# Routing moved to the beginning of a step, one sequence routed in halves, and first loads in halves, in an attention and top-1 expert kernel

## The chip, the cores and the metric

The kernel runs on one core of a Trainium2 chip. The metric is the device time of one execution in microseconds (us), as the median of several runs. All numbers of the profile come from one profiled execution of the same program.

## What is computed

Four sequences of 768 tokens with 8 heads of 64 go through an attention in which a token sees the first `n_global` (8) keys and the last `n_local` (96) keys, with a bias that grows with distance. The result, 3072 rows of 512, goes through 8 experts; each row goes to the one whose gate is highest.

```python
keep = is_global | is_local
scores = scale * q @ k.T - slopes * dist          # where keep, else -1e9
a = exp(scores - max); a = a / (sum(a) + 1e-9)
x = (a @ v) as rows of 512
logits = x @ w_gate;  e = argmax(logits);  gate_w = softmax(logits)[e]
out[row] = gate_w * (relu(x[row] @ w1[e]) @ w2[e])
```

## The kernel before

**Who orders the work.** A recorder (`Flow`) takes the instructions in the order in which the program names them, puts each into its engine's queue in that order, and derives from the tiles what each has to wait for. So each engine works its own queue strictly in program order: TensorE (PE), VectorE (DVE), ScalarE (ACT), GpSimd (POOL), and SP, which issues most DMAs. PSUM is told apart by bank: an engine that writes a bank waits for the others that read it.

**The attention as a pipeline of 24 steps.** Each sequence has 6 blocks of 128 tokens; step n (`steps`, L1087) begins block n and carries earlier blocks on. In PE's order a step has: `scores(n)` (L491, two key blocks for each query block, one for the first of a sequence), `values(n - 1)` (L528), `sums(n - 2)` (L543, the sums of the weights and the gate's logits), the transposes `q_in` and `k_in` of block n + 2 (L475, L467), `tokens_x(n - 2)` (L550) and `tokens_u(n - 2)` (L553). DVE adds the bias to the scores in two halves (`weigh`, L501), makes the logits of block n - 3 (`normal`, L562 to L566) between the two, and its rows (`rows`, L571). ACT takes exponents (L509) and copies what PE wrote: values (L531), sums (L545), and the transposed q and k (L477, L469). POOL adds the two halves of the weights (`both`, L515) and puts the first 32 keys and values of the sequence into a block (L1096, L1152). SP loads q and k four steps ahead (`loads`, L375) and v three steps ahead (`load_v`, L380).

**Routing.** When the last block of a sequence has its logits, step n with n - 3 = 5, 11, 17 ends with `choose` (L584 to L589, the best expert of each token) and `gates` (L594 to L598). In the next step, after the first `weigh`, PE counts how many earlier tokens of the sequence chose the same expert (`counts`, L605 to L610); after `rows` DVE turns that into row numbers (`slots`, L618 to L623), and six `scatter`s (L627, an indirect DMA of POOL that sends a block's 128 rows to their experts' regions) are queued, one a step; for sequence 2, whose slots come in step 21, all six are issued at the end of that step. `load_x(0)` (L779), the load of the first expert's rows, stands in SP's queue behind all scatters of sequences 0 to 2. Also in step 21 `early_counts` (L1184 and the table L733 to L743) writes down the first expert's count. Sequence 3 is routed within the first expert's products.

**Other work in the steps.** From step 5 on, eight weight loads of the first expert (L690, L693), one a step; from step 13 on eight sums of its weight quarters on DVE (`w_sums`, L710 to L713), one a step, also in steps 14 and 20, which choose.

**The beginning.** SP loads q and k of block 0 whole, then q, k and v of the next blocks. ACT's queue loads `n_global` and `n_local` spread over 128 partitions (L400, L401) and the gate weights (L419). Seven small DVE operations make floats of the two numbers (`numbers`, L389 to L395); then the masks and biases follow. Before step 0, block 0 is transposed; step 0 transposes blocks 1 and 2.

**The experts.** After step 23 (`values(23)`, the last sums) the experts' products (L842 and others) fill PE up to the end.

Of the kernel before, what the change touches and what calls it, by code (L numbers as in the profile page):

```python
# [13 lines left out]
F32 = mybir.dt.float32  # L14
BF16 = mybir.dt.bfloat16
I32 = mybir.dt.int32
# [308 lines left out]
class Attention:  # L325
# [12 lines left out]
    def __init__(self, f, dims, psum, arena, small, keep):  # L338
# [29 lines left out]
        self.top, self.se, self.slot = a.many(3, self.NBLK)  # L368

# [14 lines left out]

    def numbers(self):

        f, k = self.f, self.keep
        words, part_i, part_f, num = k["words"], k["part_i"], k["part_f"], k["num"]
        f.dve.tensor_copy(out=part_i[:, 0, :], in_=words[:, :, 1])  # L389
        f.dve.tensor_scalar(part_i[:, 1, :], words[:, :, 0], 16, None, ALU.logical_shift_right)  # L390
        f.dve.tensor_scalar(part_i[:, 2, :], words[:, :, 0], 0xFFFF, None, ALU.bitwise_and)
        f.dve.tensor_copy(out=part_f[:], in_=part_i[:])
        f.dve.tensor_scalar(num[:], part_f[:, 0, :], 4294967296.0, None, ALU.mult)
        f.dve.scalar_tensor_tensor(num[:], part_f[:, 1, :], 65536.0, num[:], ALU.mult, ALU.add)
        f.dve.tensor_tensor(num[:], num[:], part_f[:, 2, :], ALU.add)  # L395

    def constants(self):
        f, k, P, E = self.f, self.keep, self.P, self.E

        f.act.dma_start(out=k["words"][:, 0, :], in_=self.n_global.bitcast(I32).partition_broadcast(P))  # L400
        f.act.dma_start(out=k["words"][:, 1, :], in_=self.n_local.bitcast(I32).partition_broadcast(P))  # L401
# [14 lines left out]
        wg = self.w_gate.rearrange("(c p) e -> p c e", p=P)  # L416
        for a in range(2):
            r = slice(64 * a, 64 * a + 64)
            f.act.dma_start(out=self.wgbd[r, :, E * a:E * a + E], in_=wg[r])  # L419
# [14 lines left out]
    def masks(self, kinds):  # L434

        V, k = self.f.dve, self.keep
        ng, nl = k["num"][:, 0:1], k["num"][:, 1:2]
# [25 lines left out]
    def k_in(self, n, bank):  # L463
        f, pt = self.f, self.psum[:, bank, :].rearrange("p (m c) -> p m c", m=4)
        raw = self.raw_k[n % 3]
        for m in range(4):
            f.pe.transpose(pt[:, m, :], raw[:, 2 * m:2 * m + 2, :].rearrange("p a d -> p (a d)"),  # L467
                           self.keep["ident"][:])
        return lambda: f.act.copy(self.kt[n % 3], pt)  # L469

    def q_in(self, n, bank):
        f, pt = self.f, self.psum[:, bank, :].rearrange("p (m c) -> p m c", m=4)
        raw = self.raw_q[n % 3]
        for m in range(4):
            f.pe.transpose(pt[:, m, :], raw[:, 2 * m:2 * m + 2, :].rearrange("p a d -> p (a d)"),  # L475
                           self.keep["ident"][:])
        return lambda: f.act.activation(self.qt[n % 2], pt, AF.Copy, bias=0.0, scale=0.125)  # L477
# [99 lines left out]
    def choose(self, b):  # L577

        f, k, V = self.f, self.keep, self.f.dve
        xr, lg = self.xr[b % 2], self.lg[b % 2]  # L580
        shape = [128, self.NBLK, self.E]
# [1194 lines left out]
```

## Time and profile before

| | |
|---|---|
| time, median of 3 runs | 508.08 us (507.99 to 508.6) |
| profiled execution, its own time | 509.14 us |
| its span, first to last instruction | 507.3 us |
| PE, DVE, ACT, POOL busy | 94%, 70%, 34%, 32% of the span |
| mean granted TensorE clock | 0.984 |

In the profile L12 is line 12 of the kernel. `PE` is a matmul, `PEld` its weight load. A row of a timeline has its start, its length, the engine, line, operation, what it writes and reads, how many instructions it merges, and in brackets how long the engine was idle ahead of it and what ended that; "issue" there is a wait that the profile shows nothing for. A busy PE is not a PE at its peak: starts are recorded, ends are modelled. The steps can be read off PE's first L491 of each:

| step | begins at us | lasts us |
|---|---|---|
| 0, 1, 2 | 9.93, 15.54, 20.43 | 5.61, 4.88, 7.00 |
| 3, 4, 5 | 27.42, 33.67, 39.91 | 6.24, 6.24, 6.25 |
| 8, 9, 10 | 57.53, 63.77, 70.40 | 6.24, 6.63, 6.47 |
| 14, 15, 16 | 94.49, 100.73, 108.30 | 6.24, 7.56, 6.51 |
| 17, 18, 19 | 114.81, 121.05, 126.43 | 6.24, 5.38, 6.06 |
| 20, 21, 22 | 132.49, 138.73, 146.29 | 6.24, 7.56, 11.40 |
| 23 | 157.69 | 8.80 to the values of block 23 |

### The profile page before, as it was taken

Reading aid. Unit: us, or ns where it says so; the run is one execution under the profiler, and the core shown is the slowest. Engines: PE = TensorE matmul, PEld = TensorE weight load, DVE = VectorE, ACT = ScalarE, POOL = GpSimd, SP = SyncE. Lnnn points to the kernel's source line nnn. Section 1 sums busy time; section 2 is a strip of 40 time slices with the busy share of each in tenths; the row PEclk is TensorE's granted clock in tenths of the full one; section 3 lists DMA queues with packets and bytes.
Section 4 is the critical chain, followed back from the end, with each engine's and each line's share of the span. In section 5 each row is a group of like instructions: output and inputs, shape, how many; then the busy total and the mean of one; then the engine's idle time right before and its main releaser. Section 6 shows DMA issues by size and latency. Waiting matters only on the chain. (4 is left out here: it accounts for less than half of the span.)

```text
span 507.3 us, 10785 instructions
## 1 busy us (share of the span) xinstructions
PE 476.9 (94%) x4397; PEld 452.2 (89%) x4397; DVE 352.8 (70%) x626; ACT 174.0 (34%) x306; POOL 163.4 (32%) x192
## 2 busy tenths in 40 slices
PE   3999999999987999999999999999999999999990
PEld 3888888888875799999999999999999999999880
DVE  4655685898892785576868877777877776777830
ACT  3666656546543231213214214104214204303310
POOL 1545466668665143300203304303304303003011
PEclk9999999999997999999999999999999999999996
DMA  9999999999516246989756666568467479001000
GB/s 152 210 236 250 185 212 236 239 218 219 124 74 158 87 172 148 234 186 255 158 169 178 143 211 148 127 164 210 103 201 193 96 194 232 3 1 62 6 25 29
DMA packets 120344, 79.24 MB, mean 156 GB/s; under 512 B 86422, under 2 KB 103318, under 8 KB 120272
## 3 DMA queue, kind: packets, MB, share of 16 engines
q1 hardware_dynamic: 112960, 63.77, 57.6%
q0 software_dynamic: 6480, 14.45, 8.2%
q8 instruction: 51, 0.84, 0.7%
q14 instruction: 21, 0.17, 0.1%
q10 hardware_dynamic: 832, 0.02, 0.1%
HBM read 61.39 MB, written 23.71 MB: 168 GB/s over the span
## 5 line engine op out<-in xcount | busy, mean ns | idle before, releaser
L842 PE MATMUL psum<-arena 128*128 128x208 f32 (+5 forms) x1776 | 291.4, 325 | 1.1 <-DVE arena L874 0.9
L842 PEld LDWEIGHTS psum<-arena 128*128 128x128 f32 x1776 | 285.4, 190 | 3.3 <-DVE arena L874 1.9
L832 POOL DMA_INDIRECT out_dram<-arena,to x16 | 21.5, 1344 | 171.9 <-ACT arena L824 147.2
L501 DVE TENSOR_TENSOR arena<-psum,arena 128x1024 f32<-128x1024 f32 x40 | 48.8, 1219 | 36.4 <-PE psum L491 36.2
L515 POOL TENSOR_TENSOR arena<-arena 128x512 f32<-128x512 f32 x40 | 53.3, 1334 | 35.2 <-ACT arena L509 35.2
L509 ACT ACTIVATE arena<-arena 128x1024 f32<-128x1024 f32 (+1 forms) x48 | 47.4, 987 | 47.9 <-DVE arena L501 36.3
L491 PE MATMUL psum<-arena 64*128 64x128 f32 x704 | 50.4, 291 | 1.0 <-ACT arena L477 0.7
L491 PEld LDWEIGHTS psum<-arena 64*128 64x128 f32 x704 | 45.2, 198 | 5.7 <-issue 3.4
L866 ACT ACTIVATE arena<-arena 128x512 f32<-128x512 f32 x48 | 30.2, 630 | 53.4 <-DVE arena L901 21.6
L528 PE MATMUL psum<-arena 128*64 128x128 f32 x704 | 44.5, 279 | 0.3 <-issue 0.3
L528 PEld LDWEIGHTS psum<-arena 128*64 128x64 f32 x704 | 38.7, 139 | 3.3 <-issue 0.7
L870 ACT COPY arena<-psum 128x512 f32<-128x512 f32 (+1 forms) x24 | 13.5, 561 | 81.8 <-PE psum L842 81.6
L755 POOL DMA_INDIRECT xg_dram<-small,pad x24 | 23.4, 974 | 52.5 <-ACT arena L879 41.5
L627 POOL DMA_INDIRECT xg_dram<-arena,slot_i x24 | 24.7, 1030 | 23.3 <-DVE arena L911 15.8
L885 DVE TENSOR_TENSOR arena<-arena,psum 128x512 f32<-128x512 f32 (+1 forms) x24 | 15.8, 659 | 23.0 <-PE psum L842 21.0
L911 DVE TENSOR_TENSOR arena<-arena,psum 128x512 f32<-128x512 f32 x24 | 16.5, 688 | 17.7 <-PE psum L842 17.2
L906 DVE TENSOR_TENSOR arena<-arena,psum 128x512 f32<-128x512 f32 x24 | 16.5, 688 | 14.7 <-PE psum L842 13.4
L901 DVE TENSOR_TENSOR arena<-arena,psum 128x512 f32<-128x512 f32 x24 | 16.5, 688 | 12.8 <-PE psum L842 11.5
L467 PE MATMUL psum<-ident,arena 128*128 128x128 f32 x96 | 16.1, 294 | 8.8 <-DMA arena<-in_k_dram 7.3
L832 POOL DMA_INDIRECT out_dram<-ylast,to x17 | 17.4, 1024 | 21.1 <-ACT ylast L824 12.7
L713 DVE TENSOR_TENSOR arena<-arena 128x1024 f32<-128x1024 f32 x16 | 19.9, 1242 | 3.0 <-issue 2.9
L874 DVE TENSOR_TENSOR arena<-arena,psum 128x512 f32<-128x512 f32 (+1 forms) x24 | 15.8, 657 | 8.5 <-PE psum L842 8.1
(152 smaller groups left out, 534.7 us busy)
## 6 DMA issues: line engine op xcount, KB each, us to landing
arena<-in_moe_w_dram SPq DMA_DIRECT2D x64, 512.0 KB, 6.3
arena<-xg_dram SPq DMA_DIRECT2D x64, 128.0 KB, 8.5
arena<-in_q_dram SPq DMA_DIRECT2D x24, 256.0 KB, 3.5
arena<-in_k_dram SPq DMA_DIRECT2D x24, 256.0 KB, 5.1
arena<-in_v_dram SPq DMA_DIRECT2D x24, 256.0 KB, 7.7
xg_dram<-arena SPq DMA_DIRECT2D x2, 1032.0 KB
xg_dram<-arena,slot_i POOLq DMA_INDIRECT x24, 5.4
xg_dram<-small,pad POOLq DMA_INDIRECT x24, 9.3
```

The lines of the kernel that those rows point to most:

```text
L491: f.pe.matmul(self.psum[:, 2 * g + a, c:c + P], lhsT=kt[r, m, :], rhs=qt[r, m, :], start=True, stop=True, skip_group_check=True)
L501: f.dve.tensor_tensor(e, s, self.bias[:, g, :, 1:3, :].rearrange("p h k c -> p h (k c)"), ALU.add)
L509: f.act.activation(e, e, AF.Exp)
L515: f.pool.tensor_tensor(self.es[n % 3][:, g], e[:, :, 0:P], e[:, :, P:2 * P], ALU.add)
L528: f.pe.matmul(po[r, m, :], lhsT=self.v[(n - ab) % 6][:, 2 * m + a, :], rhs=self.e[n % 2][:, m // 2, 2 * a + m % 2, P * ab:P * ab + P], sta ...
L627: self.f.pool.indirect_dma_start(out=self.xs[:], out_offset=bass.IndirectOffsetOnAxis(ap=k["slot_i"][:, b % 2, u:u + 1], axis=0), in_=self ...
L713: lambda: V.tensor_tensor(c["t4"], c["b21"], c["t2"], ALU.subtract)]
L755: self.f.pool.indirect_dma_start(out=self.xs[:], out_offset=bass.IndirectOffsetOnAxis(ap=self.keep["pad"][:, g, j:j + 1], axis=0), in_=sel ...
L832: return pool.indirect_dma_start(out=self.out[:], out_offset=bass.IndirectOffsetOnAxis(ap=self.keep["to"][:, g, j:j + 1], axis=0), in_=sel ...
L842: f.pe.matmul(self.psum[:, bank, 256 * t + cut.start:256 * t + cut.stop], lhsT=w[k][:, ts(t, 128)], rhs=x[k][:, cut], start=(fresh and t = ...
L866: f.act.activation(d, d, act)
L901: V.tensor_tensor(dst["c22"], u3, bank(W), ALU.add)
```

## The change

- **Routing at the beginning of the step behind the choice.** In a step that takes slots, `normal`, `counts` and `slots` now come straight behind the scores, before the first `weigh`.
- **Sequence 2 in halves.** Its blocks 12 to 14 are chosen in step 17 and blocks 15 to 17 in step 20; slots follow in steps 18 and 21. Scatters go two a step while more than three are waiting, else one; what is left in step 21 goes ahead of that step's `both`. `early_counts` moves from step 21 to step 22. The weight sums run from step 12 on and skip the steps that choose.
- **First loads in halves.** q and k of block 0 come in four heads each, k on SP and q on ACT, and are transposed and copied in halves. The two numbers come to one partition; a matmul with ones spreads them (`near`), and the old seven operations run later, one a step, on that partition. The gate weights move from ACT's queue to SP's, behind the first v. Seven matmuls of zeros (`zeros`) go ahead of the first transposes.
- **The next blocks turned behind the scores.** Blocks 2 and 3 are transposed right behind the scores of steps 1 and 2, with ACT's copies ahead of `exponent`.

The diff, cut to what the text speaks of:

```diff
+    def first_loads(self):
+        f, k, P = self.f, self.keep, self.P
+        f.act.dma_start(out=k["words"][0:1, 0, :], in_=self.n_global.bitcast(I32).partition_broadcast(1))
+        f.sp.dma_start(out=k["words"][0:1, 1, :], in_=self.n_local.bitcast(I32).partition_broadcast(1))
+        for half in range(2):
+            r = slice(4 * half, 4 * half + 4)
+            for on, t, src in ((f.sp, self.raw_k[0], self.k), (f.act, self.raw_q[0], self.q)):
+                on.dma_start(out=t[:, r, :], in_=src[0, r, 0:P, :].rearrange("h p d -> p h d"))
+    def zeros(self, bank, count):
+        for _ in range(count):
+            self.f.pe.matmul(self.psum[:, bank, 0:self.P], lhsT=self.kg.rearrange("p a c -> p (a c)"), rhs=self.us,
+                             start=True, stop=True, skip_group_check=True)
+    def near(self, bank):
+        f, k = self.f, self.keep
+        f.dve.tensor_copy(out=self.low[0:1], in_=k["words"][0:1, :, 0])
+        f.pe.matmul(self.psum[:, bank, 0:2], lhsT=self.kg.rearrange("p a c -> p (a c)"), rhs=self.low,
+                    start=True, stop=True, skip_group_check=True)
+        f.dve.tensor_copy(out=k["near"][:], in_=self.psum[:, bank, 0:2])
...
     def constants(self):
-        f.act.dma_start(out=k["words"][:, 0, :], in_=self.n_global.bitcast(I32).partition_broadcast(P))
-        f.act.dma_start(out=k["words"][:, 1, :], in_=self.n_local.bitcast(I32).partition_broadcast(P))
+        f.dve.memset(self.kg, 1.0)
+        f.dve.memset(self.us, 0.0)
+        f.dve.memset(self.low, 0.0)
...
-        at.loads(0)
+        at.first_loads()
+        at.constants()
         at.loads(1)
         at.load_v(0)
         at.loads(2)
         at.load_v(1)
-        at.load_v(2)
-        at.constants()
+        at.gate_weights()
+        at.zeros(SK, 6)
         at.masks_first()
-        at.numbers()
-        at.k_in(0, T0)()
-        at.q_in(0, T1)()
+        at.near(SK)
+        at.zeros(SK, 1)
+        for pairs, kb, qb in ((slice(0, 2), T0, T1), (slice(2, 4), O, U)):
+            kk, qq = at.k_in(0, kb, pairs), at.q_in(0, qb, pairs)
+            kk()
+            qq()
         at.masks(slice(0, 1))
...
         at.loads(3)
+        at.load_v(2)
+        numbers = at.numbers()
+        whole, half = slice(0, NBLK), NBLK // 2
+        units = {NBLK * b + NBLK - 1: (b, whole) for b in range(B - 2)}
+        units[NBLK * (B - 2) + half - 1] = B - 2, slice(0, half)
+        units[NBLK * (B - 2) + NBLK - 1] = B - 2, slice(half, NBLK)
...
+            if n == 2:
+                kk, qq = at.k_in(3, T0), at.q_in(3, U)
+                kk()
+                qq()
-            if n + 4 < N:
+            if n + 4 < N and n != 1:
                 at.loads(n + 4)
             if n + 3 < N:
                 at.load_v(n + 3)
+            unit = routed.pop(n - 4, None)
+            if unit:
+                at.normal(n - 3, U)
+                at.counts(T1, unit[1])
+                at.slots(*unit, T1)
+                scat.extend((unit[0], u) for u in range(unit[1].start, unit[1].stop))
             at.weigh(n, 0)
+            if n == 1:
+                values_first = at.values(0, O)
+                kk, qq = at.k_in(2, U), at.q_in(2, T0)
+                kk()
+                qq()
+                at.loads(5)
             at.exponent(n, 0)
...
-            if n >= 3:
+            if n >= 3 and not unit:
                 at.normal(n - 3, U)
...
-            if n - 4 in routed:
-                at.counts(T1)
+            if n == N - 3:
+                for s in scat:
+                    at.scatter(*s)
+                scat.clear()
             at.weigh(n, 1)
             at.exponent(n, 1)
...
-            if bb is not None:
-                at.slots(bb, T1)
-                scat.extend((bb, u) for u in range(NBLK))
             us = at.sums(n - 2, U) if n >= 2 else None
-            if bb == B - 2:
+            if n == N - 2:
                 early_counts()
             kk = qq = None
-            if n + 2 < N and bb is None:
+            if 2 <= n and n + 2 < N:
                 qq = at.q_in(n + 2, T1)
-            if n + 2 < N:
                 kk = at.k_in(n + 2, SK)
             if n >= 2:
                 at.tokens_x(n - 2, T0)
-            if n + 2 < N and bb is not None:
-                qq = at.q_in(n + 2, T1)
...
+            if n >= 3 and numbers:
+                numbers.pop(0)()
...
-            if n >= 3 and (n - 3) % NBLK == NBLK - 1:
-                at.choose((n - 3) // NBLK)
-                at.gates((n - 3) // NBLK)
-                routed[n - 3] = (n - 3) // NBLK
-            if n >= 13 and w0_sums:
+            if n - 3 in units:
+                unit = routed[n - 3] = units[n - 3]
+                at.choose(*unit)
+                at.gates(*unit)
+            elif n >= 12 and w0_sums:
                 w0_sums.pop(0)()
-            for _ in range(NBLK if b == B - 1 and i >= 3 else 1):
+            for _ in range(2 if len(scat) > half else 1):
                 if scat:
                     at.scatter(*scat.pop(0))
```

`choose`, `gates`, `counts` and `slots` take the range of blocks as an argument and are otherwise the same. In step 21 the copy of the first values on POOL goes ahead of the scatters. The program that runs only when the numbers are out of range makes its own floats of them.

## Prediction, made before the change was run

> **What bounds the kernel now.** I read the slices first, then the windows of single steps, then the timelines of the engines in the one step that stands out, and the waits at the start.
>
> ```profile
> PE   3999999999987999999999999999999999999990
> PEclk9999999999997999999999999999999999999996
> ```
>
> A slice is 12.7 us. TensorE is full nearly everywhere, so the time is TensorE's queue plus its holes. There are two: the first slice, and slices 12 and 13 (140 to 165 us), where the granted clock falls too. The change touches both places. A step n begins where its scores (L491) begin on PE; these are steps 20, 21, 22, 23 (up to the values of block 23), and the half-clock stretch (columns: start:end, us, busy of each engine, clock, DMA share, GB/s).
>
> ```profile
> 132.49:138.73 6.24, 6.24 (x102) 5.58 (x101) 4.96 (x13) 3.96 (x8) 5.05 (x6) 1.00 0.13 45
> 138.73:146.29 7.56, 6.84 (x114) 5.93 (x113) 7.25 (x19) 3.32 (x6) 4.65 (x6) 1.00 0.10 37
> 146.29:157.69 11.40, 6.99 (x95) 5.13 (x94) 5.44 (x18) 4.63 (x8) 8.42 (x9) 0.93 0.37 141
> 157.69:166.49 8.80, 8.12 (x94) 7.11 (x94) 3.90 (x9) 2.75 (x4) 3.32 (x4) 0.70 0.65 120
> 156.13:162.96 6.83, 5.67 (x49) 5.23 (x51) 3.04 (x6) 2.16 (x4) 2.42 (x3) 0.50 0.77 163
> ```
>
> 6.24 us with PE busy 6.24 is the undisturbed step. Step 21, which takes slots at its end, costs 7.56; step 22 costs 11.40 although it has no transposes of q and k. In step 22 POOL issues all six scatters of sequence 2 in a row; PE and ACT stand meanwhile:
>
> ```profile
> 147.76 1.01 POOL L627 DMA_INDIRECT xg_dram<-arena,slot_i  x1 [0.81 <-DVE ki L740]
> ...
> 154.24 0.98 POOL L627 DMA_INDIRECT xg_dram<-arena,slot_i  x1 [0.30 <-issue]
> ```
> ```profile
> 155.04 0.59 ACT L531 COPY arena<-psum 128x512 f32<-128x512 f32 x1 [4.49 <-PE psum L543]
> ```
> ```profile
> 153.52 0.27 PE L543 MATMUL psum<-arena 128*32 128x128 f32 x1 [1.05 <-issue]
> 153.72 0.82 PE L550 MATMUL psum<-ident,arena 128*128 128x128 f32 x4
> 157.29 0.47 PE L553 MATMUL psum<-ident,arena 128*128 128x128 f32 x1 [2.74 <-ACT arena L545]
> 157.69 3.79 PE L491 MATMUL psum<-arena 64*128 64x128 f32 x32
> ```
>
> ACT's copy of the values waits 4.49 us for PE, although PE's records put the values' end at 150.47. Then the exponent and the sums' copy follow late, and PE's last transpose waits 2.74 us for that. The scores then take 3.79 instead of 2.06. Which part of a scatter holds PE the trace does not say; that it happens under six of them in a row, it does.
>
> At the start PE waits for the first K block, then runs long at a slow clock (16 score records in 2.08 us here, 32 in 2.06 later):
>
> ```profile
> 7.27 1.12 PE L467 MATMUL psum<-ident,arena 128*128 128x128 f32 x4 [7.27 <-DMA arena<-in_k_dram]
> 8.18 1.06 PE L475 MATMUL psum<-ident,arena 128*128 128x128 f32 x4
> 9.93 2.08 PE L491 MATMUL psum<-arena 64*128 64x128 f32 x16 [0.69 <-ACT arena L477]
> ```
>
> **What the Trainium skill says.** "TensorE: Matmul & The Clock Gate", Part 1, has the array at half clock until it was busy through a free-running window of 3.41 us, and again after an idle one. The trace agrees: half clock for 6.83 us, two windows, after PE had 1.02 us of work in 152.72 to 156.13. "SBUF — State Buffer", section "SBUF: two separate sides", says that VectorE in a two-port mode and GpSimd lock each other out of one port pair for a whole instruction. The trace agrees: the cast to slot_i (L623) took 1.14 us at 69.75, ending with POOL's sum at 70.86, and 0.17 at 181.90 with POOL idle. The same section says that TensorE never waits for a DMA at SBUF. The 4.49 us above speak at least against leaning on that. "DMA: Bandwidth & Descriptors", "Anatomy of one DMA", gives a GpSimd DMA about 2 us of completion; here the last scatter leaves POOL at 155.22 and SP's waiting load goes at 157.28.
>
> **The change, part by part.**
>
> *The six scatters of step 22 (gain).* Sequence 2 is now routed in halves: blocks 12 to 14 are chosen in step 17 and get slots in step 18; blocks 15 to 17 in steps 20 and 21. By the new rule (two scatters a step when more than three wait) the first three are out by step 20. The last three go in step 21, before the two sums on POOL, and step 22 has none. Step 22 without the stall: scores 1.98, values 1.90, sums 0.79, tokens_x 0.44, tokens_u 0.2, 5.3 on PE; but the last transpose waits for DVE, ACT: in step 4 (33.67) the sums' copy starts at +5.44, and in step 22 ACT also copies first_v (0.50), so 5.94 + 0.25, the step 6.45. Step 23 likewise 5.95. Before: 11.40 and 8.80. Gain 4.95 + 2.85 = 7.8, of which some 2.5 are the half clock (scores 1.73, values 0.73). The bounds: nothing, if the stall has another cause, and 7.8.
>
> *Slots at the beginning of a step (cost).* In steps 9, 15, 18, 21 DVE now does normal, waits for counts, does slots, and only then weigh. Behind that wait stand both weighs and rows; ACT's exponents and the sums' copy wait for them, and PE's last transpose for that copy. Counts follow the scores: 1.98 + 0.45 (67.66 to 68.11) = +2.43. Choose of the step before ends at +1.42 (65.19 against 63.77) and normal takes 0.88, to +2.3: not late. Slots 0.88 (181.12 to 181.98; the cast 0.17, since POOL has just its copy of keys then), weigh 0 at +3.3, its exponent +4.57, the values' copy +5.53, exponent 1 +6.01, the sums' copy +6.97 to +7.21, the last transpose +7.26: 7.45 in all. Before, step 9 and 10 took 6.63 + 6.47, 15 and 16 7.56 + 6.51 (one w0_sum stood ahead of their weighs), 18 5.38, 21 7.56. After: 7.45 + 6.24 twice, 5.8 (a first block, half as wide, bounded by choose and normal), 7.2 (three blocks, fewer counts). Differences +0.6, -0.4, +0.4, -0.35: +0.25. Upper bound: the cast waits for POOL each time, 4 x 0.97, +4.1; lower -0.6.
>
> *Scatters elsewhere.* Two a step: POOL 2 x 1.3 + 3.4 = 6.0, under 6.24; a sum that comes late is read two steps later. Zero. In step 21 the sums on POOL shift by 3.9 us and are read in step 23: zero. SP's load of x (7.5 us) starts at 3.3 + 3.9 + 2.0 = +9.2 in step 21 instead of 157.28 (+18.6), ready at +16.7, needed at +21: off the path both times. The early counts' table (nine small DVE operations, 146.89 to 148.24) moves to step 22, the w0_sums from steps 13 to 20 to 12 to 22. DVE in step 22: rows end +5.0, table +6.4, sum +7.5, next weigh needed at 6.45 + 1.21 = +7.66: hidden by 0.2, else their excess counts.
>
> *Start (gain).* The two words go to one partition instead of 128, gate weights behind V, q and k in halves on two queues. By +5 us the DMA engines had moved only 57 GB/s x 5 = 285 KB, then 216 KB a us. Without the small pieces I take 512 KB from 3.3 on at 216: first halves at 4.9, second at 6.1 (bounds 5.2, and 7.2 as now). Then 4 transposes of the second half, 0.9: scores(0) at 7.0 instead of 9.93 (8.1 at the bound). The near chain (one copy, matmul, copy instead of seven DVE operations of 0.2) is ready before. The seven go one a step from step 3 into DVE's idle 2.5 us: zero, 0.2 each otherwise. Seven zero matmuls wait for nothing of weight; they fill under half a window, so no clock.
>
> *The next blocks' transposes (part loss).* Blocks 2 and 3 now stand right behind the scores of steps 1 and 2, with their ACT copies ahead of exponent. From 7.0: scores 2.0, eight slow transposes 1.95, a hole of 0.8 for the copies (0.59 each), scores(1) 11.8, PE busy from there. The clock comes 3.4 to 6.8 later, 15.3 to 17 mostly. Scores(1) 3.8, values 1.0 to 1.7, transposes 1.0, hole 0.75: scores(2) 18.3 to 19.1. Scores 2.0, transposes 1.0, values 1.9, sums 0.8, transposes 0.95, the rest 0.7: scores(3) at 25.7 to 26.5, against 27.42. Gain 1.4; bounds 0.4 (loads as late as now) and 3.2 (clock by 12.8, as would be if a window four fifths full is enough).
>
> **Sum.** -7.8 + 0.25 - 1.4 = -8.95. The profiled execution took 509.14 (span 507.3, 1.8 around it), 1.06 above the median 508.08; that execution becomes 500.2, the median 499.1. From the experts on PE is full and everything only shifts.
>
> **Rivals.**
> *The stall follows the scatters* into step 21. For: three in a row remain. Against: the burst at 182.85 to 190.7 leaves PE's matmuls at their rate, and step 15 with one scatter shows none. 4.5 us over five scatters is 0.9 each: 1.8 to 2.7 for three, 499.1 + 2.7 = 501.8; with a half-clock window behind it (2.5) 504.3.
> *The start comes out well, the clock early*: 3.2 instead of 1.4, 497.3. For: the zeros and an earlier busy run. Against: 9.36 to 12.77 was over four fifths busy and did not raise the clock.
> *The change misses the cause*: step 22 stalls as before though no scatter is in it: 499.1 + 7.8 = 506.9. Against: ACT is released at 155.01, as the burst ends.
> *Slower*: the new chain counts, slots, weigh, exponent, copy, on which PE waits in four steps. Price: each us beyond my +3.3 for slots' end costs 4 us; it decides from 2.2 us a step (8.95 / 4). For: DVE's casts took 1.14 under POOL. Against: that explains 0.97, a total of +3.9 and 503.0; more is not in sight. Slower would be 510.
>
> **Chances.** Forecast as worked out, 497.8 to 500.8: 0.58. Early clock (496 to 497.8): 0.12. Stall follows, or slots cost their bound (500.8 to 504.5): 0.21. Cause missed: 0.05. Slower: 0.03; the rest ends within 0.2% (1.0 us, about what can be told from no change): 0.01. The 8-in-10 range is 496.3 to 503.2. Faster 0.95, same 0.02, slower 0.03.
>
> **What would show it.** After: no PE or ACT wait over 1 us in step 22, clock 1.00 from the warm-up to the end of attention; steps 9, 15, 21 near 7.45 with the last transpose waiting for ACT's sums' copy; slots' cast 0.17; scores(0) near 7.0, scores(3) near 26. Wrong, if step 21 holds a PE hole over 1 us under its scatters, or weigh starts after +4 in the four steps, or scores(3) is not before 27.

## The result, and the profile after

The changed kernel took 500.77 us as a median (500.38 to 501.62), the kernel before, run beside it, 508.03 (507.76 to 508.6): a ratio of 0.9858, with an interval of 0.9841 to 0.9875. The forecast was 499.1, its range 496.3 to 503.2. The profiled execution took 500.38, its span 498.5, against 509.14 and 507.3. The total came out close; its parts did not.

New line numbers for the same things: scores L519, weigh L529, exponent L537, sums on POOL L543, values L556 and their copy L559, sums on PE L571 and their copy L573, tokens_x L578, tokens_u L581, choose L612 to L616, slots L646 to L651, scatter L655, weight sums L738 to L741, the early table L761 to L771, the first expert's rows L807 and L816, its matmuls L870.

The slices first, as they were shown of before:

```profile
PE   7999999999997999999999999999999999999990
PEclk9999999999999999999999999999999999999996
```

The first slice has risen from 3 to 7 tenths, the hole in slices 12 and 13 is one slice of 7, and the clock is never taken back before the end. Then the windows of steps 20, 21, 22, 23, up to the values of block 23:

```profile
131.29:137.53 6.24, 6.24 (x102) 5.58 (x101) 4.96 (x13) 3.96 (x8) 5.04 (x6) 1.00 0.12 46
137.53:144.87 7.34, 7.00 (x109) 5.80 (x108) 6.90 (x19) 3.51 (x7) 4.77 (x6) 1.00 0.20 74
144.87:151.38 6.51, 5.66 (x95) 4.74 (x94) 5.05 (x15) 4.22 (x8) 5.87 (x6) 1.00 0.38 123
151.38:158.75 7.37, 5.72 (x95) 4.75 (x94) 5.71 (x13) 2.74 (x4) 3.80 (x4) 1.00 0.53 108
```

Step 22 is 6.51 where it was 11.40, but step 23 has PE busy for only 5.72 of 7.37. And PE's beginning (the zeros L399, the spread of the two numbers L406, the halves of k and q L495 and L503, scores of block 0):

```profile
1.42 2.93 PE L399 MATMUL psum<-arena 128*128 128x128 f32 x12 [1.42 <-DVE arena L432]
4.14 0.43 PE L406 MATMUL psum<-small,arena 128*128 128x2 f32 x2
...
5.14 0.38 PE L495 MATMUL psum<-ident,arena 128*128 128x128 f32 x2
...
6.51 1.26 PE L519 MATMUL psum<-arena 64*128 64x128 f32 x16
```

Six zeros kept PE busy for 2.93 us (a matmul of this type has two records); the clock's records show full speed from 4.63 us on (16.18 before), and the 16 score records take 1.26 us where they took 2.08.

Laid out by stages, both profiled executions:

| stretch | before | after | difference | forecast |
|---|---|---|---|---|
| start to scores(3) | 27.42 | 22.30 | -5.12 | -1.4 |
| steps 3 to 20 | 111.31 | 115.23 | +3.92 | +0.6 |
| step 21 | 7.56 | 7.34 | -0.22 | -0.35 |
| step 22 | 11.40 | 6.51 | -4.89 | -4.95 |
| step 23 | 8.80 | 7.37 | -1.43 | -2.85 |
| values(23) to the end | 340.80 | 339.78 | -1.02 | 0 |
| sum | 507.29 | 498.53 | -8.76 | -8.95 |

The +3.92 is steps 9 (7.89 for 6.63), 11 and 12 (+0.5 together), 16 (7.29 for 6.51), 17 (6.99 for 6.24) and 18 (6.12 for 5.38). So the question for the experiments is fourfold: what the start is worth and why; what the steps from 9 to 18 lose; whether the row of six scatters was the cause in step 22; and what of the tail remains. The experiments come in four groups; the kernels of one group ran on one chip. The kernel before took 507.98 to 510.19 us on these chips, so totals of different chips can't be compared: the steps in the profiles carry the verdicts, and the ratios, each against the kernel before on the same chip, support them.

### The profile page after: what moved, and what is told of

It reads as the page before. It is cut to its first block, busy times and chain, and to the rows that moved or that the text cites. A ratio compares the mean times of both kernels' runs of the same rounds, so it can differ in the third digit from the quotient of the medians.

```text
span 498.5 us, 10842 instructions
## 1 busy us (share of the span) xinstructions
PE 474.9 (95%) x4413; PEld 450.0 (90%) x4413; DVE 356.1 (71%) x646; ACT 173.2 (35%) x309; POOL 164.7 (33%) x192
## 5 line engine op out<-in xcount | busy, mean ns | idle before, releaser
L870 PE MATMUL psum<-arena 128*128 128x208 f32 (+5 forms) x1776 | 290.8, 325 | 1.0 <-DVE arena L902 0.8
L870 PEld LDWEIGHTS psum<-arena 128*128 128x128 f32 x1776 | 285.5, 190 | 2.6 <-DVE arena L902 1.3
L860 POOL DMA_INDIRECT out_dram<-arena,to x16 | 22.5, 1403 | 171.9 <-ACT arena L852 147.2
L529 DVE TENSOR_TENSOR arena<-psum,arena 128x1024 f32<-128x1024 f32 x40 | 48.3, 1219 | 29.4 <-PE psum L519 29.4
L537 ACT ACTIVATE arena<-arena 128x1024 f32<-128x1024 f32 (+1 forms) x48 | 47.4, 988 | 47.5 <-DVE arena L529 40.2
L543 POOL TENSOR_TENSOR arena<-arena 128x512 f32<-128x512 f32 x40 | 51.9, 1300 | 30.9 <-ACT arena L537 30.5
L519 PE MATMUL psum<-arena 64*128 64x128 f32 x704 | 46.4, 280 | 1.6 <-ACT arena L505 1.6
L519 PEld LDWEIGHTS psum<-arena 64*128 64x128 f32 x704 | 41.8, 187 | 5.2 <-issue 2.5
L556 PE MATMUL psum<-arena 128*64 128x128 f32 x704 | 43.7, 276 | 0.3 <-issue 0.3
L556 PEld LDWEIGHTS psum<-arena 128*64 128x64 f32 x704 | 37.9, 137 | 2.9 <-issue 0.6
L655 POOL DMA_INDIRECT xg_dram<-arena,slot_i x24 | 25.4, 1058 | 21.9 <-DVE arena L939 16.2
L741 DVE TENSOR_TENSOR arena<-arena 128x1024 f32<-128x1024 f32 x16 | 21.1, 1321 | 1.3 <-issue 1.1
L738 DVE TENSOR_TENSOR arena<-arena 128x1024 f32<-128x1024 f32 x16 | 19.4, 1211 | 1.9 <-DMA arena<-in_moe_w_dram 1.9
```

The costliest lines, as they stand in the source:

```text
L519: f.pe.matmul(self.psum[:, 2 * g + a, c:c + P], lhsT=kt[r, m, :], rhs=qt[r, m, :], start=True, stop=True, skip_group_check=True)
L529: f.dve.tensor_tensor(e, s, self.bias[:, g, :, 1:3, :].rearrange("p h k c -> p h (k c)"), ALU.add)
L537: f.act.activation(e, e, AF.Exp)
L543: f.pool.tensor_tensor(self.es[n % 3][:, g], e[:, :, 0:P], e[:, :, P:2 * P], ALU.add)
L556: f.pe.matmul(po[r, m, :], lhsT=self.v[(n - ab) % 6][:, 2 * m + a, :], rhs=self.e[n % 2][:, m // 2, 2 * a + m % 2, P * ab:P * ab + P], sta ...
L655: self.f.pool.indirect_dma_start(out=self.xs[:], out_offset=bass.IndirectOffsetOnAxis(ap=k["slot_i"][:, b % 2, u:u + 1], axis=0), in_=self ...
```

## Experiments: the two halves of the change

**start_only** is the changed kernel with the routing of before; **routing_only** the kernel before with the routing of the change (sequence 2 in halves, slots ahead of weigh, two scatters a step). start_only differs from the changed kernel by

```diff
-            unit = routed.pop(n - 4, None)
-            if unit:
-                at.normal(n - 3, U)
-                at.counts(T1, unit[1])
-                at.slots(*unit, T1)
...
+            if bb is not None:
+                at.slots(bb, whole, T1)
+                scat.extend((bb, u) for u in range(NBLK))
...
-            for _ in range(2 if len(scat) > half else 1):
+            for _ in range(NBLK if b == B - 1 and i >= 3 else 1):
```

and what belongs to it; routing_only differs from the kernel before by the same lines the other way round.

> Only the start of the change: first loads in halves, the spread of the two numbers, the zeros, blocks 2 and 3 turned behind the scores; the routing stands where it stood before (six scatters in a row in step 22). In the changed kernel's trace scores(3) begin at 22.30 us instead of 27.42. Theory (the start alone is worth 5.1 us and nothing later takes it back): scores(3) at 22.3, steps 22 and 23 at 11.4 and 8.8 as before, time 508.0 - 5.1 = 502.9. Rival (the prediction's own account, the start is worth 1.4 and the rest of what the trace shows there is given back in later steps): 506.6.

> Only the routing of the change (sequence 2 in halves, slots ahead of the first weigh, two scatters a step while more than three wait); the start stands as before. Theory (the steps from 3 to 23 took 139.07 us before and 136.45 in the changed kernel, so the routing is worth 2.6 only: 6.3 won in steps 22 and 23, 3.7 lost in steps 9 to 21): 508.0 - 2.6 = 505.4, with step 10 at 6.4, 16 at 7.3, 17 at 7.0, 22 at 6.5. Rival (the prediction's own account: 7.8 less 0.25): 500.5.

Measured: start_only 0.9942 (0.9919 to 0.9965), 507.0 us against 510.19; scores(3) at 22.62, step 22 at 12.82, step 23 at 7.84. routing_only 0.9927 (0.9910 to 0.9943), 506.25 us; step 10 at 6.48, 16 at 7.33, 17 at 7.01, 22 at 6.51.

The routing is worth 3.7 to 4 us, nearer to the theory's 2.6 than to the prediction's 7.55. The start brings scores(3) 4.8 earlier, but only 3 us of it reach the end: in this profile step 22's stall was 1.4 longer, and steps 12 and 13 took 6.16 and 6.28 instead of 5.38 and 6.0; of the first, 0.49 us are waits of PE's transposes for the loads of q and k. Such waits between scores(3) and step 23 come to 0.2 to 4.4 us in five of the ten profiles with the new start, and to 0.31 in one of the four with the old: PE has come closer to its loads, it seems. So the theory overrated what the start gives in the end, and the prediction underrated what it gives at scores(3).

## Experiment: without the zeros

```diff
-        at.zeros(SK, 6)
...
-        at.zeros(SK, 1)
```

> The changed kernel without its seven matmuls of zeros. Theory (the zeros raise the clock: they keep PE busy from 1.4 to 5, and the records show full speed from 4.63 on): without them the clock comes at 13 to 17 us, scores(3) begin at 25 to 26.5 instead of 22.3, time 503.5 to 505. Rival (the earlier loads would bring the clock anyway, or the records of the start mislead): scores(3) within 0.5 of 22.3, time 500.8 to 501.3.

Measured: 0.985 (0.9825 to 0.9875). PE's beginning in its profile:

```profile
4.26 0.69 PE L495 MATMUL psum<-ident,arena 128*128 128x128 f32 x2 [0.47 <-DMA arena<-in_k_dram]
...
6.54 2.08 PE L519 MATMUL psum<-arena 64*128 64x128 f32 x16
```

The clock came at 11.02 and scores(3) began at 23.40: neither theory. Over the nine profiles with zeros the clock came at 4.29 to 6.57 in eight and at 10.91 in one (spaced, below), though all begin with the same six zeros at 1.42. In the eight, scores(3) begin at 22.30 to 22.75, so the zeros are worth 0.7 to 1.1 us there, not 3 to 4, and the ratio can't tell the two kernels apart. In the ninth, scores(0) began at 7.25 and scores(3) at 24.02, later than without zeros.

What decides between early and late stays open. Counted back from the clock's record in stretches of 3.41 us, PE's records fill 3.15 us of the stretch that ends at 4.63 in the changed kernel. But they also fill 3.17 of 4.08 to 7.50 in spaced and 3.35 of 4.20 to 7.61 in no_zeros, and the clock stayed slow; behind the next one in no_zeros, with 2.90, it rose.

## Experiments: what steps 9 to 18 lose

In what follows a *signal* is the update of a semaphore by which PE tells a waiting engine that its matmuls are done; it is *held* when it comes late although the matmul's record has ended. In the profile of after, step 16 shows this (POOL's two scatters; ACT's copy of the values; PE's last transpose waiting for the copy of the sums):

```profile
107.29 1.02 POOL L655 DMA_INDIRECT xg_dram<-arena,slot_i  x1 [0.16 <-issue]
108.61 0.98 POOL L655 DMA_INDIRECT xg_dram<-arena,slot_i  x1 [0.30 <-issue]
110.17 0.59 ACT L559 COPY arena<-psum 128x512 f32<-128x512 f32 x1 [1.75 <-PE psum L571]
...
111.92 0.33 PE L581 MATMUL psum<-ident,arena 128*128 128x128 f32 x1 [0.39 <-ACT arena L573]
```

The values end at 108.84; their signal arrives at 110.1, half an us after the second scatter. It looks like step 22 of before on a small scale. **spaced** moves the second scatter of a pair between POOL's two sums:

```diff
             at.both(n, 0)
+            if len(scat) > half:
+                at.scatter(*scat.pop(0))
...
-            for _ in range(2 if len(scat) > half else 1):
-                if scat:
-                    at.scatter(*scat.pop(0))
+            if scat:
+                at.scatter(*scat.pop(0))
```

> The changed kernel with the same scatters in the same steps, but the second of a pair moved to POOL's queue between the two sums, so that no two stand next to each other outside step 21. Theory (PE's signals are withheld from within the first of several scatters in a row until about 0.5 us after the last; in steps 10, 11, 16 and 17 ACT's copy of the values comes 2.42, 2.51, 3.29 and 2.99 us after the values' start instead of 2.02, and those steps are 0.2, 0.3, 1.0 and 0.75 longer than 6.24): the copies return to +2.02 and the four steps to 6.24 to 6.5, time 498.3 to 499.0. Rival (these steps are long because of the new chain of counts, slots and weigh on DVE, or of the weight sums): no step moves by over 0.2, time 500.8. Second rival (each scatter holds PE by itself, so that the loss only moves to other signals of the step): 500 to 501, with the hole at the last transpose instead.

Measured: 0.9851 (0.9825 to 0.9877). Steps 10, 11, 16, 17 took 6.27, 6.24, 6.24, 6.47, and the copies came 2.28, 2.04, 2.09 and 2.24 after the values' start: as the theory had it. The total did not follow (502.27 us, forecast 498.3 to 499.0). This profile has the late clock, and its step 18 took 7.65. In that step choose's subtraction on DVE, 0.3 to 0.6 us in the other profiles, took 2.99 (from 117.81), while POOL ran two sums and a copy from 117.70 to 120.75 without a gap. From scores(3) to values(23) it came to 136.06 against 136.45: what one stall gave up, another took.

Then the changed kernel again, and **best**: sequence 0's slots at their old place, one scatter a step but for steps 15, 18, 19, and no weight sum in step 22:

```diff
...
             at.both(n, 0)
+            if n in (15, 18, 19) and scat:
+                at.scatter(*scat.pop(0))
...
-            elif n >= 12 and w0_sums:
+            elif n >= 12 and n != N - 2 and w0_sums:
                 w0_sums.pop(0)()
-            for _ in range(2 if len(scat) > half else 1):
-                if scat:
-                    at.scatter(*scat.pop(0))
+            if scat:
+                at.scatter(*scat.pop(0))
```

> The changed kernel once more, on the same chip as the next ones. All theories: 0.984 to 0.987 of the kernel before. The theory of the clock's phase (full speed comes at the end of some 3.41 us window whose place is by chance: 4.63, 5.34 and 10.91 us in three profiles with the same beginning) says that the profiled beginning may differ: scores(3) at 22.3 to 22.6 or at 24.0, and nothing in between.

> The changed kernel with sequence 0's slots back after its rows, one scatter a step (a second only in steps 15, 18, 19, between the two sums), and no weight sum in step 22. Theory (the pairs of scatters hold PE's signals and crowd POOL; the weight sum behind the early table in step 22 is what makes step 23 7.37): steps 9 to 12 take 25.0 instead of 26.43, 15 to 18 take 26.4 instead of 27.96, step 23 takes 6.7, together 3.7 less: 0.992 to 0.994 of the changed kernel. Rival (the losses of steps 9 to 18 come from the choice and slots of DVE being in more steps, whatever POOL does): steps 15 to 18 stay at 28, 0.997 to 1.0 of the changed kernel.

Measured, on one chip: changed_again 0.9875 (0.9854 to 0.9896), best 0.9828 (0.9811 to 0.9846), medians 501.33 and 498.9. best beats both the kernel before and the changed kernel; 2.4 us of the forecast 3.7 came. Steps 9 to 12 took 25.03 (forecast 25.0), step 23 6.79 (6.7), but 15 to 18 took 27.2 instead of 26.4.

The surprise is in changed_again. On this chip no signal of PE was late, pairs or not: the copies in steps 10, 11 and 16 came at +2.02, +2.02, +2.01 with both scatters where they were, and these steps took 6.24. Yet steps 17 and 18 took 7.53 and 6.74. DVE and POOL there:

```profile
109.63 4.13 DVE L741 TENSOR_TENSOR arena<-arena 128x1024 f32<-128x1024 f32 x1
```
```profile
109.62 1.28 POOL L543 TENSOR_TENSOR arena<-arena 128x512 f32<-128x512 f32 x1
110.84 0.61 POOL L1207 COPY arena<-arena 32x512 f32<-32x512 f32 x1
111.41 1.26 POOL L543 TENSOR_TENSOR arena<-arena 128x512 f32<-128x512 f32 x1
112.62 1.28 POOL L1216 COPY arena<-arena 128x128 f32<-128x128 f32 x1
```

A weight sum that takes 1.21 us elsewhere takes 4.13. As these lines read, three POOL operations without a gap go first, the sum runs from about 112.6, and now POOL's fourth, a copy of 0.3 us, has to wait and takes 1.28. Two scatters a step have made POOL late, a late POOL leaves no gaps, and DVE's sum waits for one; weigh of step 17 starts 1.6 late for it. In best the same sum took 3.90. The Trainium skill ("SBUF — State Buffer", "SBUF: two separate sides") has the shared port pair as an exclusive lock for a whole instruction of POOL against a VectorE operation with two SBUF inputs. The trace agrees, and adds that a VectorE operation can lose to three POOL instructions in a row, not to one only.

**best2** takes step 15's second scatter out of best and gives step 18 three:

```diff
+            if n == 18:
+                at.scatter(*scat.pop(0))
             at.both(n, 0)
-            if n in (15, 18, 19) and scat:
+            if n in (18, 19):
                 at.scatter(*scat.pop(0))
```

> The kernel best with the second scatter of step 15 taken out, and in step 18 one ahead of, one between and one behind the two copies that stand for sums there. In best the weight sum of step 16 took 3.90 us, from 108.50 to 112.40, while POOL ran four operations without a gap from 108.2 to 112.5; weigh of step 17 started 1.3 late for it and step 17 took 7.31. Theory (POOL with two scatters a step runs late, and a POOL without gaps shuts out VectorE's sum): step 16's sum takes 1.2 to 2, step 17 takes 6.24 to 6.5, time 0.8 to 1.0 less than best: 0.980 to 0.982 of the kernel before. Rival (step 17 is long for the choice and the weights' sum by themselves): step 17 stays at 7 to 7.5, 0.983 as best.

Measured: 0.9796 (0.9777 to 0.9815), 498.69 against 508.67. The sum of step 16 took 1.63 and step 17 6.25, as the theory of the lock had it and not its rival (7 to 7.5). POOL now leaves a gap ahead of its second sum; the weight sum goes there, and this time POOL waits:

```profile
109.88 0.60 POOL L1221 COPY arena<-arena 32x512 f32<-32x512 f32 x1
110.60 2.09 POOL L543 TENSOR_TENSOR arena<-arena 128x512 f32<-128x512 f32 x1
```
```profile
109.93 1.63 DVE L741 TENSOR_TENSOR arena<-arena 128x1024 f32<-128x1024 f32 x1
```

So on a chip that holds no signals, the lock by a late POOL is what makes step 17 long. Step 13 took 7.06, of it 1.36 us in waits for q and k. The gain over best itself can't be told from 0.9828 and 0.9796, which come from two chips.

## Experiments: the row of six, and what the tail is worth

**six_in_a_row** routes sequence 2 whole in the changed kernel; **before_apart** leaves the kernel before as it is and sets its six scatters apart.

```diff
-        units[NBLK * (B - 2) + half - 1] = B - 2, slice(0, half)
-        units[NBLK * (B - 2) + NBLK - 1] = B - 2, slice(half, NBLK)
+        units[NBLK * (B - 2) + NBLK - 1] = B - 2, whole
```
```diff
+            if n == N - 2:
+                at.scatter(*scat.pop(0))
             at.both(n, 0)
+            if n >= N - 2:
+                at.scatter(*scat.pop(0))
...
-            for _ in range(NBLK if b == B - 1 and i >= 3 else 1):
-                if scat:
-                    at.scatter(*scat.pop(0))
-            if n == N - 3:
+            if scat:
+                at.scatter(*scat.pop(0))
+            if n == N - 1:
                 ex.load_x(0, sum(tokens[:B - 1], []))
```

> The changed kernel with sequence 2 routed whole, so that all six of its scatters go in a row in step 21, ahead of its two sums; the start and everything else stay. Theory (a row of scatters withholds PE's signals to its end, whichever step it is in): PE's signals come at the end of the sixth, some 1.3 us times six behind slots: steps 21 and 22 together take 17 to 20 instead of 13.9, perhaps with a stretch of half clock behind, time 503.5 to 508. Rival (the stall of step 22 came from what else stood there, the early table or the late sums on POOL, and not from the row): steps 21 and 22 at 14 to 14.5, time 500.5 to 501.5.

> The kernel before with the six scatters of sequence 2 set apart: one at the end of step 21, one ahead of, one between and one behind the two sums of step 22, one between and one behind those of step 23, and the load of the first expert's rows behind the last. Theory (the row is what holds PE): step 22 falls from 11.4 to 6.4 to 7, step 23 from 8.8 to 6 to 7, no half clock; but the load of the rows goes some 5 us later than in the kernel before, and the first expert waits for it by up to 4 us: 501 to 506. Rival (six scatters cost the same wherever they stand): steps 22 and 23 together 18 to 20 as before, 508 to 512.

Measured, on the chip of changed_again: six_in_a_row 0.9939 (0.9920 to 0.9958), 504.65; steps 21, 22, 23 at 7.56, 6.51, 10.47. before_apart 1.0127 (1.0110 to 1.0143), 514.29; steps 22 and 23 at 6.74 and 6.56, then a wait of 10.40 us on PE for the first expert's rows, whose load started at 163.60. So the steps of before_apart are the theory's, but the time lies above both ranges: the load came later than the theory allowed for.

The totals of six_in_a_row are the theory's, the mechanism is not. No signal of PE was held, and step 22, in which four of the scatters start, is untouched. What is long is step 23: the second small operation of the early table (0.17 us elsewhere) took 5.49 us.

```profile
148.97 5.49 DVE L762 TENSOR_SCALAR inv_i<-inv 128x4 int32<-128x4 f32 x1
```
```profile
149.47 4.95 POOL L543 TENSOR_TENSOR arena<-arena 128x512 f32<-128x512 f32 x4
```

Again a late POOL without gaps, this time four sums behind the six scatters; the operation ends with the last of them. It has one SBUF input only, so it is not the case of two inputs cited above; the lines show no more than the two times. Until here the profiles of before, after and the first group had all spoken for "a row of scatters holds PE"; with these it holds only on some chips. **before_again** profiles the kernel before a second time; **six_late_table** is six_in_a_row with that table (`early_counts`) moved from step 22 to step 23, behind weigh and rows.

```diff
-            if n == N - 2:
+            if n == N - 1:
                 early_counts()
```

> The kernel before, profiled on this chip, beside the next two. In the two profiles of it or of its routing so far, PE's signals were held until the end of six scatters in a row (step 22 took 11.4 and 12.8); in four profiles of another chip no signal was held, under pairs or under six in a row. Theory A (the hold belongs to the six in a row at this place of the program): step 22 takes 11 to 13 again. Theory B (the hold comes and goes from chip to chip, and the kernel before loses as much without it, since the six scatters make POOL's sums late and VectorE waits for them): where the pairs of the other kernels here are not held, step 22 takes 6.5 to 7.5 and step 23 takes 10 to 13. The two can be told apart only if this chip shows no hold in the other kernels.

> The kernel with all six scatters in a row in step 21, and the table of the early counts moved from step 22 to step 23, behind that step's weigh and rows. In that kernel's profile the table's second small operation took 5.49 us, from 148.97 to 154.46, while POOL ran the four late sums from 149.47 to 154.42 without a gap, and step 23 took 10.47. Theory (POOL's late sums shut VectorE's small operation out; nothing else in step 22 or 23 minds them): the two steps take 13 to 14 together instead of 16.98, no half clock behind them, time 498 to 501 where it was 504.65 (0.981 to 0.987 of the kernel before). Rival (six scatters in a row cost this by the hold of PE's signals or the lateness of the sums themselves): 16 to 18 together, 503 to 506. On a chip that holds PE's signals the hold adds some 4 to both.

before_again (one run, 508.04 us) answers the first question. Nothing was held; step 22 took 6.73, step 23 6.57, and then PE stood:

```profile
157.10 3.78 SPq L779 DMA_DIRECT2D arena<-xg_dram  x8
160.92 1.81 SPq L788 DMA_DIRECT2D gt<-xg_dram  x2
165.32 0.16 DVE L795 TENSOR_TENSOR to<-gt,is_i 128x4 int32<-128x4 int32 x1 [4.63 <-DMA gt<-xg_dram]
...
167.00 3.68 PE L842 MATMUL psum<-arena 128*128 128x256 f32 x8 [4.16 <-DVE arena L806]
```

This is neither of its theories: no 11 to 13 in step 22, and no 10 to 13 in step 23. The loss moved. SP's load of the first expert's rows starts behind the sixth scatter, at about the same time in both profiles of before. In the first, the hold kept PE from the first expert until 169.80, and the rows were there:

```profile
157.28 3.79 SPq L779 DMA_DIRECT2D arena<-xg_dram  x8
...
169.80 1.89 PE L842 MATMUL psum<-arena 128*128 128x256 f32 x8
```

In the second PE is there at 162.8 and waits until 167.00, and the clock is at half for the next 3.41 us:

```profile
163.73:167.14 3.41, 0.14 (x1) 0.14 (x2) 1.77 (x4) 0.00 (x0) 0.00 (x0) 1.00 0.03 3
167.14:170.55 3.41, 3.41 (x8) 2.25 (x8) 3.27 (x8) 0.00 (x0) 0.00 (x0) 0.50 0.00 0
```

six_late_table: 0.9938 (0.9920 to 0.9955), the same as six_in_a_row: the time (505.01) and the two steps (16.34 together) are the rival's. Its profile still confirms half of the theory. Weigh of step 23 was on time (157.63, 1.28 behind the scores' start; 5.11 in six_in_a_row), but PE's last transpose then waited 3.29 us for the table (its operation took 1.74 under POOL's sums), because that table now came later than the point where the program needs the expert's size; step 23 took 9.83. It doesn't show what six scatters would cost with neither. This profile is of the slowest of its 16 runs (510.22 us; median 505.01): 4.36 us of waits for q and k, ahead of step 14, are in it. And before_apart, read beside before_again, points to the load once more: its steps 22 and 23 are the same, its load starts 6.5 us later, and PE waits 6.24 longer.

In the changed kernel the load starts earlier, and PE does not wait:

```profile
149.24 3.79 SPq L807 DMA_DIRECT2D arena<-xg_dram  x8
...
162.06 1.89 PE L870 MATMUL psum<-arena 128*128 128x256 f32 x8
```

**rows_late** is the direct test of the load: the last three scatters, and the load behind them, go to the end of step 22.

```diff
-            if n == N - 3:
-                for s in scat:
-                    at.scatter(*s)
-                scat.clear()
...
-            for _ in range(2 if len(scat) > half else 1):
+            for _ in range(0 if n == N - 3 else half if n == N - 2 else 2 if len(scat) > half else 1):
                 if scat:
                     at.scatter(*scat.pop(0))
-            if n == N - 3:
+            if n == N - 2:
                 ex.load_x(0, sum(tokens[:B - 1], []))
```

> The changed kernel with the last three scatters of sequence 2 (blocks 15 to 17) at the end of step 22 instead of in step 21; SP's load of the first expert's rows, which has to wait for them, goes with them. Theory (that load is on the path as soon as it starts about a step later; in the kernel before the 4.5 us of PE's stall hid it, and where nothing stalled PE waited 4.16 us for the rows instead): the load starts at 157 to 159 instead of 149.24, the first expert's matmuls at 166.5 to 168 instead of 162.06, time 505 to 507, 0.993 to 0.997 of the kernel before. Rival (the prediction's words, the load is off the path both times): the first expert's matmuls within 0.5 of 162.06, time 500.5 to 501.5, 0.985 to 0.988.

Measured: 1.004 (1.0023 to 1.0056), 510.56 against 508.18. Its profile, after a step 22 of 6.51 and a step 23 of 7.50 (6.51 and 7.37 in the changed kernel):

```profile
158.85 4.60 SPq L807 DMA_DIRECT2D arena<-xg_dram  x8
163.49 1.22 SPq L816 DMA_DIRECT2D gt<-xg_dram  x2
166.56 0.16 DVE L823 TENSOR_TENSOR to<-gt,is_i 128x4 int32<-128x4 int32 x1 [6.52 <-DMA gt<-xg_dram]
...
168.23 3.78 PE L870 MATMUL psum<-arena 128*128 128x256 f32 x8 [4.44 <-DVE arena L834]
```

The theory holds, and understated it: 9.6 us later in the load, 6.2 later in the first expert (168.23 for 162.06), and with the half clock that follows the whole gain of the change is gone.

## Why the prediction was right, and where it was not

The likeliest case was within 1.7 us of the median, and within 0.2 of the profiled execution (500.2 for 500.38). That is luck in part, because its misses cancel: 3.7 us more from the start, 3.3 us more lost in steps 3 to 20; step 23 gave 1.4 less, and 1.0 after it was not foreseen at all (the experts' matmuls are the same ones; 0.6 of it came in small jumps between 200 and 460 us, whose cause is open). And the two profiled executions flatter it: by the medians the gain was 7.26 us of the forecast 8.95.

*The six scatters of step 22.* The forecast of 6.45 for step 22 was right (6.51); PE's longest wait there is 0.51 us and the clock stayed (ACT still waits 1.22 us once, for the scores). But the cause given, PE standing under scatters in a row, is only half of it. Two of the chips show it, in the small also under pairs; the other profiles, on three chips, show none, six in a row included. The kernel before takes about as long on both kinds of chip (508.03 and 510.19 us with the hold, 507.98 to 508.67 without), because the late rows wait behind the hold. "Off the path both times" is the sentence that failed. It is true of the two profiles that it compares, but the load was hidden by the very stall that the change removed. From the start of step 22 to the first expert's matmul it took 23.5 us with the hold, 20.95 in before_again, 17.2 in the changed kernel and 23.5 again in rows_late. That the load starts at 149.24 instead of 157.28 is therefore part of the gain, not a side effect.

Where nothing is held, this is all that the routing gains. Between before_again and changed_again (one profile each, from two chips) the stretch to scores(3) falls from 27.25 to 22.58, steps 3 to 23 grow from 132.11 to 135.92, and what follows the values of block 23 falls from 346.73 to 340.32, of it 4.33 up to the first expert's matmul. Steps 22 and 23 together took 13.30 and 13.73: on such a chip the 7.8 us of the prediction aren't there, and the total comes out alike for another reason. What in a chip or a placement makes the hold stays open; no run tried it.

*Step 23.* "Hidden by 0.2" failed: the table took 1.95 us (149.82 to 151.77) instead of 1.4, one of its operations 0.69 under POOL's sum, and the weight sum behind it 1.66 instead of 1.21. Weigh of step 23 began 0.7 late, and PE waited for rows:

```profile
150.01 0.69 DVE L761 TENSOR_TENSOR inv<-cnt,slot 128x4 f32<-128x4 f32 x1
151.69 1.66 DVE L741 TENSOR_TENSOR arena<-arena 128x1024 f32<-128x1024 f32 x1
153.27 1.21 DVE L529 TENSOR_TENSOR arena<-psum,arena 128x1024 f32<-128x1024 f32 x1
```
```profile
157.14 0.66 PE L578 MATMUL psum<-ident,arena 128*128 128x128 f32 x4 [1.01 <-DVE arena L599]
```

Without the weight sum (best) the step took 6.79, so that was 0.58 of the 1.42; the rest is that 5.95 was too low a base: without transposes in the step, tokens_x and tokens_u wait for rows and the copy each time (0.41 and 0.23 us in best).

*Slots at the beginning.* The chain is as described and each link took its forecast time, the cast 0.17. Its beginning was off, by a term that the prediction put at zero: one of the seven operations of the numbers stands ahead of choose in step 8.

```profile
57.37 0.49 DVE L419 SCALAR_TENSOR_TENSOR num<-part_f,num 1x2 f32<-1x2 f32 x1
58.25 1.17 DVE L614 SCALAR_TENSOR_TENSOR small<-small,rev 128x48 f32<-128x48 f32 x1
```

So gates ended at +1.94 (counted as in the prediction, to the next instruction's start) instead of +1.42, weigh began at +3.68 instead of +3.3, and step 9 took 7.89 instead of 7.45. Choose's third operation, under POOL's second sum, adds little to that, since in before the fifth (L588) had taken 0.95 in its place. routing_only, which has no such operation in step 8, took 7.56 for step 9. Step 21 took 7.34 (7.2), step 18 6.12 (5.8).

*"Scatters elsewhere: zero".* This is the cost that failed most: "POOL 2 x 1.3 + 3.4 = 6.0, under 6.24". The sum leaves no room for POOL's own waits, and asks only whether the results of POOL come in time. They do. What costs is what a busy POOL does to others: PE's signals held (steps 10, 11, 16, 17 in the profile of after) or DVE locked out (step 17 of changed_again, step 18 of spaced).

*Start.* "They fill under half a window, so no clock" failed on a size: a zero takes 0.49 us at the slow clock and six take 2.93, most of 3.41. And "15.3 to 17" failed without the zeros too: the clock came at 11.02. The mechanism of the loads was right, scores(0) at 6.51 (7.0), though the prediction's figures (512 KB at 216 KB a us, from 3.3 on) give 4.5 and 5.7 for the two halves and not its 4.9 and 6.1; PE's transposes of them began at 5.14 and 5.58.

The slower rival (each us of late slots costs 4) didn't come: weigh was 0.38 late in step 9, far under its 2.2. The rival of the hold following into step 21 didn't either: three scatters ended at 146.89, and the longest wait of PE in step 21 is 0.29 us.

## What to carry to other kernels

When a stall goes, ask what it had been hiding: list everything that was ready "in time" only because PE was late, and give each its time without the stall. And a POOL that is filled to 96% of a step is not free: its queue loses its gaps, and VectorE operations like the ones shown here then wait for a gap, so that work on POOL should be priced by the gaps that it leaves. Where a total is forecast well, check its parts before believing the reasons.

## What the runs showed that was not expected

PE's signals under scatters are held on some chips and not on others: within the attention a signal came up to 4.8 us behind the start of its matmul's record in before, 6.2 in start_only, 2.5 in after, 1.8 in routing_only, and in the eight profiles of the last three groups never over 0.7. The traces' records of these updates split the same way: 386 to 391 for PE's 406 or 408 signalling instructions in the six profiles of the first two chips, spaced included, and 408 or 410 in the other eight. The time of the kernel before doesn't tell the two apart.

The same six zeros were followed by full speed at 4.3 to 6.6 us eight times and at 10.9 once. The Trainium skill ("TensorE: Matmul & The Clock Gate", Part 1) gives the transition as about 4 us into sustained work with half an us to either side. Counted from the first zero at 1.42 it took 2.9 to 5.2 us here, and 9.5 in the one, which cost 1.3 to 1.7 us at scores(3). Nor was PE idle where the clock was taken back: its records fill 1.02 of the 3.41 us ahead of the half clock in before, which the prediction took for agreement with an idle window, and 1.95 in no_zeros (157.80 to 161.21).
